# Retention attention and a Mish MLP on one core: q and k of the first two tiles by batch, a quarter of w_in on another queue, G2 of tile 0 moved up

## The chip, the core and the metric

The kernel runs on one core of a Trainium2 chip. The core has five engines, each with its own instruction queue that runs in order: TensorE (PE, matrix products; its weight loads are PEld), VectorE (DVE), ScalarE (ACT), GpSimd (POOL) and SyncE (SP, which only issues transfers here). Transfers between the chip's memory and the core's on-chip memory (DMAs) are issued by SP, POOL or ACT and are carried out by 16 DMA engines. Matrix results go to PSUM, eight banks of 128 partitions x 2 KB.

The metric is the device time of one execution in microseconds (us). Before the change it is 351.88 us, the median of 3 runs (351.87 to 352.25).

## The reference

Eight batches, eight heads, 576 positions, head size 64. Attention with a decay, no softmax; then an MLP over all 4608 tokens.

```python
scores = scale * np.matmul(q, k.transpose(0, 1, 3, 2))
Dmat = np.where(rel >= 0, gamma[:, None, None] ** rel[None, :, :], 0.0)
attn = np.matmul(scores * Dmat, v)                   # 8, 8, 576, 64
x = attn.transpose(0, 2, 1, 3).reshape(4608, 512)
h = x @ w_in                                         # 512 x 2048
out = (h * np.tanh(softplus(h))) @ w_out             # Mish, 2048 x 512
```

## The kernel before

Tokens are cut into 36 chunks of 128, and four chunks make a tile: nine tiles, t = 0 to 8. Tiles 0 and 1 hold chunk 0 of each of the eight batches, which needs no earlier state and has a path of its own. Chunk n >= 8 (N0 = 8) is a later chunk of a batch and takes its past from a running state.

For a tile, G1 (`g1`, 16 calls of 4 products of 128x128 by 128x512) computes h from w_in, and ACT applies Mish into `gT`. G2 (`g2`, 16 calls of 4 products) multiplies `gT` by w_out: four groups s of 128 tokens, each in four parts of w_out. The result is copied to `res` and stored (`store`). I call a call of `g1` or `g2`, four products, a unit.

The program orders every instruction by hand (`manual_schedule`): each engine's queue is the order in which Python emits it. What counts around the change:

- **First tiles.** `load_first(t)` fetches q and k of four batches into `stage` (name gT) by 16 DMAs of 128 KB, one per head and tensor, over all 128 partitions, then four v DMAs of 256 KB; all on SP. `f_cast` makes bf16 of a pair of heads (8 per tile), `f_transpose` turns it on PE through PSUM, `f_scores` multiplies and DVE applies the decay, `f_v` casts v, `f_out` multiplies by v into `xT`, `f_state` scales v for the state (POOL) and `f_k` reorders k inside on-chip memory by four DMAs per batch on SP. For tile 0 `keep_warm` puts products of zeros between them.
- **Weights.** `load_w_in(i)` and `load_w_out(i)` load a quarter each (1 MB read, 512 KB written as bf16) on POOL's queue. The second `load_first` waits for a write into `stage` behind tile 0's output (L433).
- **Order of the tiles.** G1 of tile 0 (L355) has the transposes and scores of tile 1 between its units from f = 6 on; then `f_out` of tile 1; then five chunk loads; G1 of tile 1; G2 of tile 0 with the attention of chunks 8 to 11 (tile 2); and from there a loop over t = 2 to 8 in which unit i of G1 of tile t and unit i of G2 of tile t - 1 take turns, with the attention of the next tile between them.
- **Chunks.** `load(n)` issues k on POOL (cast to bf16 on its way) and q, v on SP. The steps: P scales q (DVE), V scales v (POOL, L264), T transposes q and k, S computes the scores (L286) and masks them on DVE, `state` updates the running state, O adds the state's part and the chunk's own (L336, L341). T runs on PE with a copy by ACT for n < NPE = 12, and as a DMA transpose issued by SP (L276) from n = 12 on.
- **Buffers.** `io` has five (PF) of qraw and of vraw; `hp` two banks, `sc` two of two banks, `st` and `ops` one each; `res` three.

Of the kernel before, what the change touches and what calls it, by code (L numbers as in the profile page):

```python
# [17 lines left out]
def kernel(  # L18
# [25 lines left out]
    nF = d_ff // P  # L44
    KC = d_model // P
    NCH = 4
    NPE = 12
    PF = 5


# [44 lines left out]
    v0 = {}  # L95

    def load_first(t):
        for p in range(NP):
            for dst, src in ((qf, q), (kf, k)):
                for h in (2 * p, 2 * p + 1):  # L100
                    nc.sync.dma_start(  # L101
                        out=dst[:, h, :],
                        in_=src[ds(4 * t, 4), h, 0:P, :].rearrange("b (g r) d -> g b (r d)", r=4))
        for b in range(4 * t, 4 * t + 4):
            v0[b] = io.tile([P, H, D], F32, name="vraw")
            nc.sync.dma_start(out=v0[b], in_=v[b, :, 0:P, :].rearrange("h p d -> p h d"))

    load_first(0)

    zeros = consts.tile([P, 512], BF16)  # L110
    nc.vector.memset(zeros, 0.0)  # L111
# [64 lines left out]
    def f_transpose(t, p, copies):  # L176
        if t == 0:
            tps = [ps_h.tile([P, 4, P], BF16, name="hp") for _ in range(2)]
        else:
            both = ps_sc.tile([P, 2, 8, P], BF16, name="sc")  # L180
            tps = [both[:, i, 0:4] for i in range(2)]
        for i, name in enumerate(("qb", "kb")):
            out_t = first.tile([P, 4, P], BF16, name=name + "T", bufs=2)
            for r in range(4):
                nc.tensor.transpose(tps[i][:, r, :],
                                    fst[t][name][:, r, ds(2 * p, 2), :].rearrange("p h d -> p (h d)"), ident)
            copies[i](out_t.rearrange("p b (g r) -> p b g r", r=4),
                      tps[i].rearrange("p r (g b) -> p b g r", b=4))
            fst[t][name, p] = out_t

    def f_scores(t, p):
# [16 lines left out]
    def f_out(t, b, copy):  # L208
        if b == 0:
            xts[t] = xp.tile([P, KC, NCH * P], BF16, name="xT")  # L210
        vb = fst[t]["vb"][b]
        pool, name = ((ps_st, "st"), (ps_o, "ops"))[b % 2]
        ot = pool.tile([P, NP, P], F32, name=name)
        for p in range(NP):
            for e in range(2):
                nc.tensor.matmul(ot[ds(64 * e, 64), p, :], lhsT=vb[:, 2 * p + e, :],
                                 rhs=fst[t]["sm", p][:, e, b, :],
                                 start=(p == 0), stop=True, skip_group_check=True)
        copy(xts[t][:, :, ts(b, P)], ot)
# [7 lines left out]
    def f_k(t, b):  # L227
        n = 4 * t + b
        k0[n] = first.tile([P, H, D], BF16, name="k0", bufs=B)
        for r in range(4):  # L230
            nc.sync.dma_start(out=k0[n][ds(r, 32, step=4)].rearrange("p h d -> p (h d)"),  # L231
                              in_=fst[t]["kb"][ds(b, 32, step=4), r].rearrange("p h d -> p (h d)"))

    def load(n):
        if n >= n_chunks:
            return
        b, c = chunks[n]
        qr = io.tile([P, H, D], F32, name="qraw")  # L240
        vr = io.tile([P, H, D], F32, name="vraw")
        qks = io.tile([P, 2, H, D], BF16, name="qks", bufs=9)
        live[n] = {"q": qr, "v": vr, "qks": qks}
        if n == N0:
            nc.vector.memset(qr[0:1, 0, 0:1], 0.0)
        for t, src, queue in ((qks[:, 1], k, nc.gpsimd), (qr, q, nc.sync), (vr, v, nc.sync)):
            if c < 4:
                queue.dma_start(  # L248
                    out=t, in_=src[b, :, ds(P * c, P), :].rearrange("h p d -> p h d"))
            else:  # L250
                for e in range(2):
                    queue.dma_start(
                        out=t[ds(64 * e, 64)],
                        in_=src[b + e, :, ds(512, 64), :].rearrange("h p d -> p h d"))

# [103 lines left out]
    def g2(t, i):  # L359
        s, part = divmod(i, 4)  # L360
        if t == nT - 1:
            s = (s + 3) % 4
        if part == 0:
            if (t == nT - 1 or t == 0) and s % 2:
                outs[t] = ps_h.tile([P, d_model], F32, name="hp")
            else:
                outs[t] = ps_o.tile([P, d_model], F32, name="ops")
        ops = outs[t]
        for f in range(4 * part, 4 * part + 4):
            nc.tensor.matmul(ops, lhsT=gts[t][:, f, ts(s, P)], rhs=w_out_t[:, f, :],  # L370
                             start=(f == 0), stop=(f == nF - 1))
        if part == 3:
            store(t, s, ops, nc.scalar.copy if t == 0 else nc.vector.tensor_copy)

    def g2_last(t, s):
        b, c = chunks[NCH * t + s]
# [26 lines left out]
    dve, act, pool = nc.vector.tensor_copy, nc.scalar.copy, nc.gpsimd.tensor_copy  # L403


    f_cast(0, 0, 0, dve)
    f_cast(0, 0, 1, pool)
    for p in range(1, NP):
        f_cast(0, p, 0, pool)
        f_cast(0, p, 1, pool)  # L410
        if p == 2:
            make_masks()
    load_w_in(0)
    keep_warm(8)
    for p in range(NP + 1):
        if p < NP:
            f_transpose(0, p, (act, act))
            keep_warm(3)
        if p > 0:
            f_scores(0, p - 1)  # L420
            keep_warm(2)
    f_v(0, 0, pool)
    f_v(0, 1, act)
    load_w_in(1)
    f_v(0, 2, pool)
    f_v(0, 3, dve)
    for b in range(4):
        f_out(0, b, (dve, act)[b % 2])
        if b < 3:
            keep_warm_b = 0  # L430
    load_w_in(2)
    load_w_in(3)
    nc.vector.memset(stage[0:1, 0, 0, 0:1], 0.0)  # L433
    load_first(1)
    for b in range(4):
        f_state(0, b)
        f_k(0, b)
    for i in range(4):
        load_w_out(i)


    for p in range(NP):
        f_cast(1, p, 0, pool)
        f_cast(1, p, 1, pool)
    for b in range(4):
        f_v(1, b, pool)
    for b in range(4):
        f_state(1, b)
        f_k(1, b)
    for f in range(nF):  # L450
        if f in (6, 8, 10, 12):
            f_transpose(1, (f - 6) // 2, (dve, dve))
        if f in (8, 10, 12, 14):
            f_scores(1, (f - 8) // 2)
        g1(0, f)
    for b in range(4):
        f_out(1, b, dve)


    for n in range(N0, N0 + PF):  # L460
        load(n)
    for f in range(nF):
        g1(1, f)
        if f == 8:
            state(N0)
    att(N0, "PV")
    for i in range(nF):
        n, w = N0 + i // 4, i % 4
        if w == 0:
            att(n, "T")  # L470
        elif w == 1:
            if i > 4:
                att(n - 1, "O")
        elif w == 2:
            att(n, "S")
            state(n + 1)
        else:
            att(n + 1, "PV")
            load(n + PF)
            state(n + 1)  # L480
        g2(0, i)
    att(3 * NCH - 1, "O")
    queued = [3 * NCH + PF - 1]

    def more_loads(upto):
        for _ in range(2):
# [4 lines left out]
    for t in range(2, nT + 1):  # L491
        for i in range(nF):
            n, w = NCH * (t + 1) + i // 8 * 2, i % 8
            if t == nT:
                pass
            elif n == 3 * NCH:
                steps = {0: ((n, "T"), (n + 1, "PV")), 1: ((n + 1, "T"), (n, "K")),
                         3: ((n, "S"), (n + 1, "S"), (n + 1, "K")), 2: ((n + 2, "PV"),), 4: ((n + 3, "PV"),),
                         6: ((n + 1, "K"), (n, "O"), (n + 1, "O"), (n + 3, "K"), (n + 2, "T")),
                         7: ((n + 3, "T"),)}  # L500
                for m, step in steps.get(w, ()):
                    if step == "K":
                        state(m)
                        continue
                    att(m, step)
                    if step == "PV":
                        more_loads(m + PF)
            else:
                if w == 0:
                    att(n, "S")  # L510
                    att(n + 1, "S")
                    state(n + 1)
                if w in (0, 2):
                    att(n + 2 + w // 2, "PV")
                    more_loads(n + 2 + w // 2 + PF)
                elif w in (1, 3):
                    att(n + 2 + w // 2, "T")
                elif w == 4:
                    state(n + 3)
                    att(n, "O")  # L520
                    att(n + 1, "O")
                    state(n + 3)
                elif w == 6:
                    state(n + 3)
            if t < nT:
                g1(t, i)
            if t < nT or i < 12:
                g2(t - 1, i)
    g2_last(nT - 1, 2)

# [29 lines left out]
```

## Time and profile before

One execution was profiled. Its instructions span 352.2 us, and it took 353.91 us with what lies around them; the runs without a profile have the median 351.88.

| | busy us | share of the span |
|---|---|---|
| PE | 311.0 | 88% |
| ACT | 130.5 | 37% |
| DVE | 110.0 | 31% |
| POOL | 86.7 | 25% |

| group | count | mean |
|---|---|---|
| G1 products, L355 | 546 | 390 ns |
| G2 products, L370 | 492 + 61 | 381, 379 ns |
| Mish, L357 | 144 | 597 ns |
| score mask, L290 | 28 | 1216 ns |
| chunk T copied by ACT, L274 | 4 | 1015 ns |

Of the 41 us in which PE has nothing to do, most lie ahead of 150 us. A product's 390 ns is not its cost: products are pipelined, and a unit of four follows the last by 0.86 us. "DMA" in the slices of the page is the mean busy share of the 16 DMA engines, and a name such as `DMA qkT<-qks` is a transfer by its target and source.

### The profile page before, as it was taken

The numbers are of one execution on the slowest core, as the hardware profiler recorded it, in microseconds if no ns is written. First come the engines' busy times: TensorE is split into PE (matmuls) and PEld (weight loads), VectorE is DVE, ScalarE is ACT, GpSimd is POOL, SyncE is SP. The second block draws the span as 40 slices with busy tenths as digits, with TensorE's granted clock in tenths as the row PEclk, the third lists the DMA queues.
The fourth block names the chain that finished last, engine by engine and source line by source line (L and its number), as shares of the span: only waits on it lengthen the run. The fifth ranks groups of instructions, "written<-read, shape, count | busy, mean of one in ns | idle before, by whom it ended". The sixth has DMA issues, their size and how long they took to land.

```text
span 352.2 us, 5825 instructions
## 1 busy us (share of the span) xinstructions
PE 311.0 (88%) x2342; PEld 152.0 (43%) x2380; DVE 110.0 (31%) x156; ACT 130.5 (37%) x241; POOL 86.7 (25%) x112
## 2 busy tenths in 40 slices
PE   5927678979970999999999999999999999999995
PEld 2413333435430445444544445454545454444444
DVE  2330364014521352424252525244242423200021
ACT  7414132745420244353434344343435243333300
POOL 4682249017451144040404031320201000000000
PEclk9987898999996799999999999999999999999999
DMA  4999974989999999995979788991723220020022
GB/s 148 212 202 216 257 171 67 111 162 203 214 223 203 188 134 181 123 191 92 180 126 147 164 117 170 130 173 68 152 44 78 67 54 30 32 58 33 30 61 89
DMA packets 140123, 46.65 MB, mean 132 GB/s; under 512 B 126144, under 2 KB 135616, under 8 KB 140096
## 3 DMA queue, kind: packets, MB, share of 16 engines
q1 hardware_dynamic: 105504, 38.16, 51.0%
q0 software_dynamic: 34448, 8.00, 26.5%
q8 instruction: 18, 0.29, 0.4%
q10 hardware_dynamic: 144, 0.13, 0.1%
q14 instruction: 9, 0.07, 0.1%
HBM read 37.49 MB, written 9.44 MB: 133 GB/s over the span
## 4 chain that ended last, share of the span: by engine, by line
PE 66%; DMA 17%; SPq 11%; issue 2%; ACT 2%; DVE 1%; POOL 0%; ACTq 0%; DVEq 0%; POOLq 0%
PE ops L370 28%; PE hp L355 25%; DMA qkT<-qks 8%; SPq L231 6%; DMA gT<-in_q_dram 5%; PE hp L370 4%; SPq L101 4%; DMA vraw<-in_v_dram 3%; PE sc L286 2%; PE st L318 2%; ACT ssb L322 1%; PE sc L336 1%; DMA qraw<-in_q_dram 1%; PE sc L341 1%; PE hp L381 1%
## 5 line engine op out<-in xcount | busy, mean ns | idle before, releaser
L355 PE MATMUL hp<-xT,w_in_t 128*128 128x512 bf16 x546 | 145.8, 390 | 5.3 <-issue 2.2
L357 ACT ACTIVATE gT<-hp 128x512 bf16<-128x512 f32 x144 | 86.0, 597 | 149.2 <-PE hp L355 143.6
L370 PE MATMUL ops<-w_out_t,gT 128*128 128x512 bf16 x492 | 126.8, 381 | 0.4 <-PE st L318 0.2
L355 PEld LDWEIGHTS <-w_in_t 128*128 128x128 bf16 x576 | 55.1, 100 | 68.7 <-issue 9.3
L370 PEld LDWEIGHTS <-gT 128*128 128x128 bf16 x560 | 54.1, 98 | 64.7 <-issue 1.9
L389 DVE COPY res<-ops 128x512 f32<-128x512 f32 x29 | 20.1, 692 | 147.0 <-PE ops L370 140.4
L264 POOL TENSOR_TENSOR vs<-vraw,gv 128x512 bf16<-128x512 f32 x28 | 29.3, 1048 | 148.0 <-issue 89.7
L322 ACT ACTIVATE ssb<-st,diag 128x256 bf16<-128x256 f32 x64 | 26.8, 470 | 34.2 <-PE st L318 34.2
L290 DVE TENSOR_TENSOR sm<-sc,mask 128x1024 bf16<-128x1024 f32 x28 | 33.1, 1216 | 18.7 <-PE sc L286 18.7
L258 DVE TENSOR_TENSOR qks<-qraw,gq 128x512 bf16<-128x512 f32 x28 | 18.2, 682 | 18.0 <-DMA qraw<-in_q_dram 18.0
L248 POOL DMA_DIRECT2D qks<-in_k_dram x25 | 23.1, 931 | 2.2 <-PE st L318 2.2
L345 DVE CAST xT<-sc 128x512 bf16<-128x512 f32 x28 | 18.2, 686 | 10.7 <-PE sc L341 10.6
L286 PE MATMUL sc<-qkT 64*128 64x128 bf16 x224 | 10.0, 224 | 10.6 <-DMA qkT<-qks 10.6
L370 PE MATMUL hp<-w_out_t,gT 128*128 128x512 bf16 x61 | 14.7, 379 | 0.4 <-issue 0.3
L286 PEld LDWEIGHTS <-qkT 64*128 64x128 bf16 x224 | 6.5, 96 | 18.1 <-DMA qkT<-qks 11.7
L160 PE MATMUL ops<-zeros 128*128 128x512 bf16 x27 | 11.0, 529 | 1.3 <-DVE zeros L111 1.3
L199 DVE TENSOR_TENSOR sm<-sc,dmask 128x1024 bf16<-128x1024 f32 x8 | 9.7, 1218 | 7.7 <-PE sc L197 7.7
L336 PE MATMUL sc<-qkT,ssb 128*64 128x128 bf16 (+1 forms) x256 | 11.2, 215 | 0.0
L341 PE MATMUL sc<-sm,vs 128*64 128x128 bf16 x224 | 10.9, 219 | 0.0
L336 PEld LDWEIGHTS <-ssb 128*64 128x64 bf16 x256 | 7.8, 111 | 2.5 <-issue 2.5
L225 POOL TENSOR_TENSOR v0s<-vraw,gv 128x512 bf16<-128x512 f32 x8 | 8.4, 1072 | 1.5 <-DMA vraw<-in_v_dram 1.5
L318 PE MATMUL st<-vs,qks 128*64 128x64 bf16 x192 | 7.7, 202 | 1.0 <-ACT ssb L322 0.5
(71 smaller groups left out, 116.5 us busy)
## 6 DMA issues: line engine op xcount, KB each, us to landing
vraw<-in_v_dram SPq DMA_DIRECT2D x33, 256.0 KB, 4.5
out_dram<-res SPq DMA_DIRECT2D x31, 256.0 KB, 2.1
qraw<-in_q_dram SPq DMA_DIRECT2D x25, 256.0 KB, 3.7
qks<-in_k_dram POOLq DMA_DIRECT2D x25, 128.0 KB, 5.7
gT<-in_q_dram SPq DMA_DIRECT2D x16, 128.0 KB, 5.0
gT<-in_k_dram SPq DMA_DIRECT2D x16, 128.0 KB, 4.3
w_in_t<-in_moe_w_in_dram POOLq DMA_DIRECT2D x4, 512.0 KB, 9.6
w_out_t<-in_moe_w_out_dram POOLq DMA_DIRECT2D x4, 512.0 KB, 13.8
```

What stands on the lines that cost most here:

```text
L231: nc.sync.dma_start(out=k0[n][ds(r, 32, step=4)].rearrange("p h d -> p (h d)"), in_=fst[t]["kb"][ds(b, 32, step=4), r].rearrange("p h d -> ...
L248: queue.dma_start(out=t, in_=src[b, :, ds(P * c, P), :].rearrange("h p d -> p h d"))
L258: nc.vector.tensor_tensor(live[n]["qks"][:, 0], live[n]["q"], gq[:, c, :].unsqueeze(2).to_broadcast([P, H, D]), op=OP.mult)
L264: nc.gpsimd.tensor_tensor(vs, live[n]["v"], gv[:, c, :].unsqueeze(2).to_broadcast([P, H, D]), op=OP.mult)
L286: nc.tensor.matmul(sc[:, e, p, :], lhsT=qk[r, 1, p, :], rhs=qk[r, 0, p, :], start=True, stop=True)
L290: nc.vector.tensor_tensor(sm.rearrange("p e n i -> p (e n) i"), sc.rearrange("p e n i -> p (e n) i"), m.unsqueeze(1).to_broadcast([P, 2 * ...
L322: nc.scalar.activation(ssb[:, :, e, :], st, AX.Copy, scale=diag[:, e:e + 1])
L336: nc.tensor.matmul(ot[ds(64 * e, 64), p, ds(i0, iw)], lhsT=st_sb[bb, cc][:, p, e, :], rhs=qk[:, 0, p, ds(i0, iw)], start=(i0 == 0 and p == ...
L355: nc.tensor.matmul(hp, lhsT=w_in_t[:, c, ts(f, P)], rhs=xts[t][:, c, :], start=(c == 0), stop=(c == KC - 1))
L357: nc.scalar.activation(gts[t][:, f, :], hp, AX.Mish)
L370: nc.tensor.matmul(ops, lhsT=gts[t][:, f, ts(s, P)], rhs=w_out_t[:, f, :], start=(f == 0), stop=(f == nF - 1))
L389: copy(ot, ops)
```

## The change

- Of tiles 0 and 1, q and k are fetched by half of the heads, by tensor and by batch: 16 DMAs of 128 KB, each into 32 partitions. The rows of a tile are then ordered by batch, so the transposes' copies read `(b g)` instead of `(g b)`, and `f_k` is one DMA per batch instead of four.
- The first quarter of w_in comes in f32 by four DMAs on SP after v of tile 0, into free qraw buffers, and DVE casts it. The other three stay on POOL.
- q, k of tile 1 are issued on SP behind that, with no write that holds them back. v of tile 1 is issued on POOL.
- Tile 0's q casts go to DVE for even pairs; tile 1's eight casts go to DVE. Fewer `keep_warm`.
- G1 of tile 0 runs without anything in it. G2 of tile 0 follows at once (`g2_first`): by part of w_out first, then by group s, with four open results in `hp`, `hp`, `ops`, `st`; tile 1's transposes and scores lie between its units. Then `f_v` and `f_out` of tile 1.
- G1 of tile 1 and the first half of G2 of tile 1 (24 units) then have the attention of chunks 8 to 11 between them. The loop at t = 2 has 16 units of G1 and the 8 that remain of G2 of tile 1.
- NPE is 16: chunks 12 to 15 are transposed on PE too.
- All chunk loads (q, k, v) are issued on POOL.

```diff
-    NPE = 12
+    NPE = 16
     def load_first(t):
-        for p in range(NP):
+        for half in range(2):
+            hs = ds(4 * half, 4)
             for dst, src in ((qf, q), (kf, k)):
-                for h in (2 * p, 2 * p + 1):
+                for b in range(4):
                     nc.sync.dma_start(
-                        out=dst[:, h, :],
-                        in_=src[ds(4 * t, 4), h, 0:P, :].rearrange("b (g r) d -> g b (r d)", r=4))
+                        out=dst[ds(32 * b, 32), hs, :],
+                        in_=src[4 * t + b, hs, 0:P, :].rearrange("h (g r) d -> g h (r d)", r=4))
...
+            (nc.gpsimd if t else nc.sync).dma_start(out=v0[b], in_=v[b, :, 0:P, :].rearrange("h p d -> p h d"))
     load_first(0)
+    load_first_v(0)
+    w0 = []
+    for c in range(KC):
+        w0.append(io.tile([P, 512], F32, name="qraw"))
+        nc.sync.dma_start(out=w0[c], in_=w_in_r[:, c, 0:512])
...
-        for r in range(4):
-            nc.sync.dma_start(out=k0[n][ds(r, 32, step=4)].rearrange("p h d -> p (h d)"),
-                              in_=fst[t]["kb"][ds(b, 32, step=4), r].rearrange("p h d -> p (h d)"))
+        nc.sync.dma_start(out=k0[n].rearrange("p h d -> p (h d)"),
+                          in_=fst[t]["kb"][ds(32 * b, 32)].rearrange("p r h d -> p r (h d)"))
...
-        for t, src, queue in ((qks[:, 1], k, nc.gpsimd), (qr, q, nc.sync), (vr, v, nc.sync)):
+        for t, src in ((qr, q), (qks[:, 1], k), (vr, v)):
             if c < 4:
-                queue.dma_start(
+                nc.gpsimd.dma_start(
...
+    def g2_first(part, s):
+        if part == 0:
+            pool, name = ((ps_h, "hp"), (ps_h, "hp"), (ps_o, "ops"), (ps_st, "st"))[s]
+            outs[0, s] = pool.tile([P, d_model], F32, name=name)
+        for f in range(4 * part, 4 * part + 4):
+            nc.tensor.matmul(outs[0, s], lhsT=gts[0][:, f, ts(s, P)], rhs=w_out_t[:, f, :],
+                             start=(f == 0), stop=(f == nF - 1))
+        if part == 3:
+            store(0, s, outs[0, s], nc.scalar.copy if s % 2 else nc.vector.tensor_copy)
...
+    load_first(1)
     keep_warm(8)
...
+    for i in range(1, 4):
+        load_w_in(i)
     for b in range(4):
         f_out(0, b, (dve, act)[b % 2])
+        dve(w_in_t[:, b, 0:512], w0[b])
...
     for p in range(NP):
-        f_cast(1, p, 0, pool)
-        f_cast(1, p, 1, pool)
+        f_cast(1, p, 0, dve)
+        f_cast(1, p, 1, dve)
+    for f in range(nF):
+        g1(0, f)
     for b in range(4):
+        f_k(1, b)
+    load(N0)
+    first_steps = {0: (f_transpose, 0), 1: (f_transpose, 1), 3: (f_scores, 0), 4: (f_scores, 1),
+                   6: (f_transpose, 2), 7: (f_transpose, 3), 9: (f_scores, 2), 11: (f_scores, 3)}
+    for i in range(nF):
...
+        g2_first(i // 4, i % 4)
+    for b in range(4):
+        f_v(1, b, act if b % 2 else pool)
+    for b in range(4):
+        f_out(1, b, (dve, act)[b % 2])
+    for b in range(4):
+        f_state(1, b)
+        load(N0 + 1 + b)
+    att(N0, "PV")
+    for u in range(24):
+        j, w = divmod(u, 4)
...
+        elif w == 3 and j < 4:
+            att(N0 + j, "T")
...
+        if u < nF:
+            g1(1, u)
+        else:
+            g2(1, u - nF)
...
+            if t == 2:
+                if i % 2:
+                    g2(1, 8 + i // 2)
```

More of the change, by code (lines that the diff above doesn't have):

```diff
@@ L97, in load_first, with load_first_v @@
     def load_first(t):
-        for p in range(NP):
+        for half in range(2):
+            hs = ds(4 * half, 4)
             for dst, src in ((qf, q), (kf, k)):
-                for h in (2 * p, 2 * p + 1):
+                for b in range(4):
                     nc.sync.dma_start(
-                        out=dst[:, h, :],
-                        in_=src[ds(4 * t, 4), h, 0:P, :].rearrange("b (g r) d -> g b (r d)", r=4))
+                        out=dst[ds(32 * b, 32), hs, :],
+                        in_=src[4 * t + b, hs, 0:P, :].rearrange("h (g r) d -> g h (r d)", r=4))
+    def load_first_v(t):
         for b in range(4 * t, 4 * t + 4):
             v0[b] = io.tile([P, H, D], F32, name="vraw")
-            nc.sync.dma_start(out=v0[b], in_=v[b, :, 0:P, :].rearrange("h p d -> p h d"))
+            (nc.gpsimd if t else nc.sync).dma_start(out=v0[b], in_=v[b, :, 0:P, :].rearrange("h p d -> p h d"))
     load_first(0)
+    load_first_v(0)
[3 more added lines that the diff above has]
+        nc.sync.dma_start(out=w0[c], in_=w_in_r[:, c, 0:512])
     zeros = consts.tile([P, 512], BF16)
@@ L187, in f_transpose @@
             copies[i](out_t.rearrange("p b (g r) -> p b g r", r=4),
-                      tps[i].rearrange("p r (g b) -> p b g r", b=4))
+                      tps[i].rearrange("p r (b g) -> p b g r", b=4))
             fst[t][name, p] = out_t
@@ L211, in f_out @@
         vb = fst[t]["vb"][b]
-        pool, name = ((ps_st, "st"), (ps_o, "ops"))[b % 2]
-        ot = pool.tile([P, NP, P], F32, name=name)
+        if t == 0:
+            pool, name = ((ps_st, "st"), (ps_o, "ops"))[b % 2]
+            ot = pool.tile([P, NP, P], F32, name=name)
+        else:
+            if b % 2 == 0:
+                fst[t]["ot"] = ps_sc.tile([P, 2, NP, P], F32, name="sc")
+            ot = fst[t]["ot"][:, b % 2]
         for p in range(NP):
@@ L243, in load @@
         live[n] = {"q": qr, "v": vr, "qks": qks}
-        if n == N0:
-            nc.vector.memset(qr[0:1, 0, 0:1], 0.0)
-        for t, src, queue in ((qks[:, 1], k, nc.gpsimd), (qr, q, nc.sync), (vr, v, nc.sync)):
+        for t, src in ((qr, q), (qks[:, 1], k), (vr, v)):
             if c < 4:
-                queue.dma_start(
+                nc.gpsimd.dma_start(
                     out=t, in_=src[b, :, ds(P * c, P), :].rearrange("h p d -> p h d"))
@@ L251, in load @@
                 for e in range(2):
-                    queue.dma_start(
+                    nc.gpsimd.dma_start(
                         out=t[ds(64 * e, 64)],
@@ L363, in g2 @@
         if part == 0:
-            if (t == nT - 1 or t == 0) and s % 2:
+            if t == nT - 1 and s % 2:
                 outs[t] = ps_h.tile([P, d_model], F32, name="hp")
@@ L372, in g2 @@
         if part == 3:
-            store(t, s, ops, nc.scalar.copy if t == 0 else nc.vector.tensor_copy)
+            store(t, s, ops, nc.vector.tensor_copy)
+    def g2_first(part, s):
[7 more added lines that the diff above has]
+            store(0, s, outs[0, s], nc.scalar.copy if s % 2 else nc.vector.tensor_copy)
     def g2_last(t, s):
@@ L403 @@
     dve, act, pool = nc.vector.tensor_copy, nc.scalar.copy, nc.gpsimd.tensor_copy
[L406 to L409, printed above, removed]
+    for p in range(NP):
+        f_cast(0, p, 0, pool if p % 2 else dve)
         f_cast(0, p, 1, pool)
-        if p == 2:
-            make_masks()
-    load_w_in(0)
+    load_first(1)
     keep_warm(8)
@@ L417 @@
             f_transpose(0, p, (act, act))
-            keep_warm(3)
+            keep_warm(2)
         if p > 0:
             f_scores(0, p - 1)
-            keep_warm(2)
     f_v(0, 0, pool)
     f_v(0, 1, act)
-    load_w_in(1)
     f_v(0, 2, pool)
-    f_v(0, 3, dve)
+    f_v(0, 3, act)
+    for i in range(1, 4):
+        load_w_in(i)
     for b in range(4):
         f_out(0, b, (dve, act)[b % 2])
[L429 to L434, printed above, removed]
+        dve(w_in_t[:, b, 0:512], w0[b])
     for b in range(4):
@@ L439 @@
         load_w_out(i)
+    load_first_v(1)
+    make_masks()
     for p in range(NP):
-        f_cast(1, p, 0, pool)
-        f_cast(1, p, 1, pool)
+        f_cast(1, p, 0, dve)
+        f_cast(1, p, 1, dve)
+    for f in range(nF):
+        g1(0, f)
     for b in range(4):
-        f_v(1, b, pool)
+        f_k(1, b)
+    load(N0)
+    first_steps = {0: (f_transpose, 0), 1: (f_transpose, 1), 3: (f_scores, 0), 4: (f_scores, 1),
+                   6: (f_transpose, 2), 7: (f_transpose, 3), 9: (f_scores, 2), 11: (f_scores, 3)}
@@ L447 @@
+    for i in range(nF):
+        if i in first_steps:
+            step, p = first_steps[i]
+            if step is f_transpose:
+                step(1, p, (dve, act))
+            else:
+                step(1, p)
+        g2_first(i // 4, i % 4)
[3 more added lines that the diff above has]
+        f_out(1, b, (dve, act)[b % 2])
     for b in range(4):
         f_state(1, b)
[L449 to L465, printed above, removed]
+        load(N0 + 1 + b)
     att(N0, "PV")
-    for i in range(nF):
-        n, w = N0 + i // 4, i % 4
+    for u in range(24):
+        j, w = divmod(u, 4)
         if w == 0:
[L470 to L476, printed above, removed]
-        else:
[L478 to L481, printed above, removed]
@@ L482 @@
-    att(3 * NCH - 1, "O")
-    queued = [3 * NCH + PF - 1]
+            if 0 < j:
+                att(N0 + j, "PV") if j < 5 else None
+                load(N0 + j + PF - 1) if j < 5 else None
+            if 2 <= j < 6:
+                att(N0 + j - 2, "O")
+        elif w == 3 and j < 4:
+            att(N0 + j, "T")
+        elif w == 1 and 1 <= j < 5:
+            att(N0 + j - 1, "S")
+            state(N0 + j - 1)
+        elif w == 2 and j < 5:
+            state(N0 + max(j - 1, 0))
+        if u < nF:
+            g1(1, u)
+        else:
+            g2(1, u - nF)
@@ L485, in more_loads @@
+    queued = [3 * NCH + PF]
     def more_loads(upto):
@@ L526 @@
                 g1(t, i)
-            if t < nT or i < 12:
+            if t == 2:
+                if i % 2:
+                    g2(1, 8 + i // 2)
+            elif t < nT or i < 12:
                 g2(t - 1, i)
```

## The prediction

> **What bounds the kernel now.** First the slices of the page, to see where PE, the busiest engine, is not full: up to the 17th of 40 slices, some 150 us; behind them it is at 9 throughout.
>
> ```profile
> PE   5927678979970999999999999999999999999995
> PEclk9987898999996799999999999999999999999999
> ```
>
> Then the stages, PE's busy time in three windows. The loop over t = 2 runs from 98.55 to 143.58; the next two lines are whole tiles (32 units each).
>
> ```profile
> 98.55:143.58 45.03, 34.52 (x268) 16.57 (x271) 12.28 (x16) 13.74 (x26) 13.20 (x15) 0.89 1.30 185
> 143.58:176.97 33.39, 32.18 (x262) 15.83 (x266) 12.27 (x16) 13.74 (x26) 8.25 (x9) 1.00 0.93 143
> 160.74:193.13 32.39, 31.68 (x261) 15.69 (x265) 12.26 (x16) 12.91 (x24) 8.19 (x9) 1.00 1.02 140
> ```
>
> A tile costs 32.4 us and is PE all through. In the chain of waits a unit takes 0.86 us, so 32 units are 27.6 and a tile's attention 4.8. At t = 2 the same work takes 45.0: 12.6 are lost. Third, PE's timeline, for what it waited for ("[idle before <-who ended it]"):
>
> ```profile
> 25.01 0.64 PE L216 MATMUL st<-sm,vb 128*64 128x128 bf16 x8 [5.32 <-DVE xT L219]
> ...
> 27.55 6.29 PE L355 MATMUL hp<-xT,w_in_t 128*128 128x512 bf16 x22 [0.22 <-issue]
> 35.56 0.40 PE L185 MATMUL sc<-ident,qb 128*128 128x128 bf16 x4 [1.72 <-POOL qb L173]
> ...
> 76.19 0.62 PE L273 MATMUL sc<-ident,qks 128*128 128x128 bf16 x8 [2.64 <-DVE qks L258]
> ...
> 109.01 0.61 PE L286 MATMUL sc<-qkT 64*128 64x128 bf16 x8 [5.12 <-DMA qkT<-qks]
> 114.36 0.61 PE L286 MATMUL sc<-qkT 64*128 64x128 bf16 x8 [4.74 <-DMA qkT<-qks]
> ```
>
> The 12.6 are two DMA transposes, with the half clock that follows (0.55 from 110 to 120). The front is another matter: from 26.75 to 57.5 PE does one G1 (13.8 us of units) and tile 1's first attention, and waits for tile 1's q and k. Last, SP's and POOL's queues, for why data come late:
>
> ```profile
> 47.95 22.96 SPq L231 DMA_DIRECT2D k<-kb  x32
> 71.01 1.57 SPq L248 DMA_DIRECT2D qraw<-in_q_dram  x1
> ```
>
> 32 small DMAs hold SP for 23 us, and the first chunk's q is issued only at 71.
>
> **The change, part by part.** All times are on the profiled execution.
>
> *Tile 0's loads.* Still 16 q, k DMAs of 128 KB, one per 0.64 us, 2.6 to 2.9 us from issue to landing: the first half of k lands at 8.1, the last k at 13.2. What 32 partitions cost in place of 128 the trace does not show. From below, nothing: the issue is the limit. From above, twice the 0.64: 10.3 us. The nearest row, 128 KB into 64 partitions (L252, 3.4 us to landing, against 3.7 for 256 KB into 128), shows a small load as no slower, so I take 0 and leave the 10.3 to a rival.
>
> [...]
>
> POOL's last cast moves from 13.95 to 15.1 (kb, then qb, kb at 0.61 after 13.2), a loss of 1.1 that lies beside v.
>
> *v and w_in.* v lands at 14.9, 16.2, 17.3 and only 23.9 for the fourth, because w_in's DMAs issued from 13.90 on take the engines. Now w_in waits on POOL for the third v's cast (17.9), so the fourth v lands one step later, 18.5. The first w_in quarter follows on SP: a quarter alone takes 2.55 (landings 25.0 to 30.1, two steps), shared at most twice that: 21.0 to 23.6, I take 22.5. DVE's casts are four at 0.43 (row L173), the last behind the landing. G1 of tile 0 starts at 23, not 26.75.
>
> *Weights and tile 1's q, k share the engines from 22.5 on.* In the trace, sharing, a quarter took 4.1 (w_out, 33.9 to 46.3) and a q or k DMA 0.92 (33.4 to 47.2, 15 steps), 1.1 in its middle. So w_in's last three land at 25, 29 and 33, the last k between 37 and 40, w_out at 37, 40, 42.5 and 45, v of tile 1 at 1.2 each by 50. G1 of tile 0 ends 3.45 (four units) after 33, at 37 with a little for the clock, which was at 0.68 from 20 to 30.
>
> *G2 of tile 0.* 16 units 13.8, four transposes at 0.45, four scores at 0.33: 16.9. DVE's queue has all eight casts of tile 1 ahead of the first qbT copy, so the first scores wait for the last k, three casts (1.3) and 0.69: 39 to 42, where PE would come at 40.5. I take 1. End: 55. Before, this was not done at 57.5.
>
> *To G1 of tile 1.* The fourth result's copy by ACT needs a third `res` back, whose store left some 2 us earlier (landings 2.1 in the median): a wait of 0 to 1.6. Behind it on ACT lie two vb casts (0.63) and two xT copies (0.59), and G1 waits for the last: 0.6 + 1.3 + 1.2 + 1.6 = 4.7. Start 60, where before it was 57.5. So 16 units, 13.8, are won here and 2.5 given back. At this place the clock fell for some 3.4 us before (0.88 in 50 to 60); I keep that, 1.7.
>
> *24 units with attention.* 20.7 + 4.8 + four transposes 1.8 = 27.3. ACT has in four units four Mish (0.597), a copy of 1.015 and a state (0.84): 4.2 of PE's 5.1; it fits, but bunched, with two `hp` banks. Cost 0 to 4 (one copy per chunk); I take 1.5. The 2.64 at 76 has gone, for q no longer stands behind `f_k`. End: 60 + 1.7 + 27.3 + 1.5 = 90.5.
>
> *Loads on POOL.* Three issues per chunk:
>
> ```profile
> L248 POOL DMA_DIRECT2D qks<-in_k_dram x25 | 23.1, 931 | 2.2 <-PE st L318 2.2
> L264 POOL TENSOR_TENSOR vs<-vraw,gv 128x512 bf16<-128x512 f32 x28 | 29.3, 1048 | 148.0 <-issue 89.7
> ```
>
> 2.8 + 1.05 is 3.85 of the 8.1 us that a chunk takes PE. At the start it is tight: from 49 POOL has four v0s and four loads, one of which waits for ACT's vb (58), then vs of chunks 8 and 9, at 67 and 68. PE needs the first in O of chunk 8, eight units and some attention after 61.7: 70. Cover 3; without it every us counts.
>
> *t = 2.* 16 + 8 units 20.7, attention 4.8, four PE transposes 1.8 for the 12.6 lost: 27.3 and 0.5 for small gaps. End 118.3, where before it was 143.58: 25.3 less. Behind it the order is the old one and already full; SP carries less there. I take 0; from below -1 (the gaps from 143.58 to 176.97 against the tile after), from above +3 (a transposed chunk late, as the 0.50 at 144.48, at each tile).
>
> **Sum.** 352.2 - 25.3 = 326.9. The median of the runs is 0.3 below the profiled span, so 327 (the profiled execution itself, 353.91, would be near 329). With no cold clock, no bunching and no wait for `res` or k it is 6 less: 320.5; with k and w_out 3 late and 4 for ACT, 334.
>
> **Rivals.**
>
> *The front is late.* Each us that tile 1's last k or w_out comes after 41 delays G2 of tile 0. For: queues there were full before (mean share above 1). Against: the bytes up to 50 are the same, and v no longer stands in w_in's way. With half the rate into 32 partitions tile 0 is 10.3 later, 337, and part of tile 1's 16 times 0.92 more comes on top: 334 to 346, at 340.
>
> *Only the transposes' stall goes.* If PE with G1 and attention waits as long as G2's early units gained, 12.6 less 1.8 remain: 341.4. For: two banks, a fuller ACT. Against: 4.2 of 5.1.
>
> *POOL becomes the bound, and it is slower than before.* All loads stand in order behind V's waits. From 50 on POOL has 28 chunks, and 60 us follow the last scores (291.6 of 352.2). It passes 352 once a chunk takes (352 - 110)/28 = 8.65, an issue 2.5 us. At 3 us an issue: 50 + 28 x 10.05 + 60 = 391. Against: 0.93 in 25 rows, and 4.46 for five in a row.
>
> **How the numbers follow.** Forecast 0.66 (own range 320 to 334), late front 0.20, transposes only 0.06, POOL 0.07, no change 0.01. The range 320 to 341 holds the forecast, two thirds of the late front and little of the rest: near 0.8. Within 0.2% is what a measurement of this kernel can't tell from no change. Faster: 0.66 + 0.20 + 0.06 = 0.92; same 0.01; slower 0.07.
>
> **What would show it.** G1 of tile 0 starts near 23 and ends near 37; G2 of tile 0 ends near 55; G1 of tile 1 starts near 60; no PE wait for qkT of 4 to 5 us remains; the t = 2 loop takes some 28; PE's busy time stays near 311 and its idle falls from 41 to some 16. Wrong, if POOL's issues take over 1.5 us, if q or k of tile 1 lands after 45, or if whole tiles behind 120 take more than 33.

## The result, and the profile after

The changed kernel takes 334.53 us, the median of 4 runs (333.42 to 335.18), beside 352.06 us (351.87 to 352.66) of the kernel before on the same chip. The ratio is 0.950, with the interval 0.947 to 0.953. The profiled execution took 335.18 us and its instructions span 333.5. PE's busy time hardly moved (311.0 to 309.7); its idle time fell from 41 to 24 us, not to 16.

The slices of the page:

```profile
PE   5839788699999999999999999999999999999996
PEclk9969999879999999999999999999999999999999
```

A slice is 8.3 us here. PE is full from the ninth slice on, some 67 us, where before it was from the fourteenth, some 115 (its row reads 7 and 0 in the 12th and 13th slice and 9 from there; the prediction's 17th and 150 are misread). The long dip of the old loop over t = 2 has gone. What is left lies in the first eight slices.

The stages, in three windows of busy time (start and end, length; then PE, PEld, DVE, ACT and POOL, each with its count, PE's granted clock, the DMA share and GB/s). The first holds the 24 units with the attention of chunks 8 to 11, the second the loop over t = 2, the third a whole tile:

```profile
67.28:97.78 30.50, 30.22 (x264) 14.69 (x264) 12.31 (x14) 16.80 (x30) 26.93 (x31) 0.94 0.95 165
97.78:126.12 28.34, 27.82 (x281) 14.67 (x280) 11.57 (x15) 18.01 (x32) 20.15 (x23) 1.00 0.83 133
126.12:158.83 32.71, 32.42 (x266) 15.82 (x266) 12.26 (x16) 13.74 (x26) 14.90 (x16) 1.00 1.10 164
```

The loop over t = 2 took 45.03 before and takes 28.34 now: 8 of its units moved ahead (6.9 us) and 9.8 us more are gone, the waits less the four added PE transposes. In all three stages PE is busy all but half a microsecond. So most of the time by which the kernel misses the forecast lies ahead of 67. PE's timeline there:

```profile
23.33 12.15 PE L365 MATMUL hp<-xT,w_in_t 128*128 128x512 bf16 x48 [3.23 <-DVE xT L232]
...
41.49 0.38 PE L193 MATMUL sc<-ident,kb 128*128 128x128 bf16 x4 [1.75 <-DVE qbT L195]
...
43.81 0.38 PE L193 MATMUL sc<-ident,kb 128*128 128x128 bf16 x4 [0.85 <-DVE qbT L195]
...
50.39 0.38 PE L193 MATMUL sc<-ident,kb 128*128 128x128 bf16 x4 [0.78 <-DVE qbT L195]
...
52.65 0.38 PE L193 MATMUL sc<-ident,kb 128*128 128x128 bf16 x4 [0.78 <-DVE qbT L195]
...
64.14 1.05 PE L229 MATMUL sc<-sm,vb 128*64 128x128 bf16 x16 [2.12 <-ACT vb L213]
...
67.28 3.57 PE L365 MATMUL hp<-xT,w_in_t 128*128 128x512 bf16 x8 [0.67 <-ACT xT L232]
```

Four times in G2 of tile 0 PE comes to k's transposes and waits for DVE to have copied q's out of the same `sc` tile. These four are 4.2 us, the largest group of waits in the profile. The first is longer than the others because DVE's queue has three of tile 1's casts, behind the last k's landing at 39.6, ahead of that copy:

```profile
39.74 0.43 DVE L181 CAST kb<-gT 128x512 bf16<-128x512 f32 x1 [4.03 <-DMA gT<-in_k_dram]
...
40.76 0.68 DVE L195 COPY qbT<-sc 128x512 bf16<-128x512 bf16 x1
```

Then PE waits 2.1 us for v's cast by ACT. The last row of PE's timeline is a half clock (0.50 granted from 64.2 to 71.0): eight products took 3.57 us, where they take 1.89 at full clock.

SP's and POOL's queues, at the places that were shown of before:

```profile
31.87 11.49 SPq L243 DMA_DIRECT2D k<-kb  x8
```

```profile
L258 POOL DMA_DIRECT2D qks<-in_k_dram x24 | 21.6, 899 | 3.0 <-DMA w_out_t<-in_moe_w_out_dram 3.0
```

The reordering of k holds SP for 11.5 us instead of 23, and POOL's issues cost 0.90 to 0.93 us, as before.

### The profile page after: what moved, and what is told of

Read it like the earlier page. It is cut to its first block, busy times and chain, and to the rows that moved or that the text cites. A ratio compares the mean times of both kernels' runs of the same rounds, so it can differ in the third digit from the quotient of the medians.

```text
span 333.5 us, 5849 instructions
## 1 busy us (share of the span) xinstructions
PE 309.7 (93%) x2400; PEld 151.5 (45%) x2400; DVE 117.2 (35%) x162; ACT 137.6 (41%) x252; POOL 136.0 (41%) x167
## 4 chain that ended last, share of the span: by engine, by line
PE 81%; DMA 9%; SPq 3%; DVE 2%; ACT 2%; issue 1%; DVEq 0%; ACTq 0%
PE hp L365 34%; PE ops L380 30%; DMA gT<-in_k_dram 6%; PE st L328 3%; PE sc L296 2%; PE hp L380 2%; PE hp L391 2%; DMA qraw<-in_moe_w_in_dram 2%; ACT ssb L332 2%; SPq L102 1%; DMA gT<-in_q_dram 1%; PE sc L346 1%; SPq L109 1%; PE hp L402 1%; PE sc L283 1%
## 5 line engine op out<-in xcount | busy, mean ns | idle before, releaser
L365 PE MATMUL hp<-xT,w_in_t 128*128 128x512 bf16 x576 | 147.6, 386 | 4.3 <-DVE xT L232 3.2
L367 ACT ACTIVATE gT<-hp 128x512 bf16<-128x512 f32 x144 | 86.1, 598 | 126.1 <-PE hp L365 124.6
L380 PE MATMUL ops<-w_out_t,gT 128*128 128x512 bf16 x464 | 117.9, 379 | 0.3 <-DVE res L410 0.3
L365 PEld LDWEIGHTS <-w_in_t 128*128 128x128 bf16 x576 | 53.8, 99 | 67.5 <-issue 4.0
L380 PEld LDWEIGHTS <-gT 128*128 128x128 bf16 x496 | 48.3, 98 | 58.4 <-issue 1.0
L258 POOL DMA_DIRECT2D qraw<-in_q_dram x24 | 22.4, 933 | 54.0 <-DVE qks L268 52.2
L274 POOL TENSOR_TENSOR vs<-vraw,gv 128x512 bf16<-128x512 f32 x28 | 29.7, 1074 | 12.6 <-PE sc L351 12.4
L332 ACT ACTIVATE ssb<-st,diag 128x256 bf16<-128x256 f32 x64 | 26.8, 470 | 16.9 <-PE st L328 16.9
L258 POOL DMA_DIRECT2D vraw<-in_v_dram x24 | 21.8, 908 | 6.0 <-issue 3.3
L258 POOL DMA_DIRECT2D qks<-in_k_dram x24 | 21.6, 899 | 3.0 <-DMA w_out_t<-in_moe_w_out_dram 3.0
L268 DVE TENSOR_TENSOR qks<-qraw,gq 128x512 bf16<-128x512 f32 x28 | 20.5, 767 | 0.0
L262 POOL DMA_DIRECT2D qraw<-in_q_dram x8 | 5.6, 703 | 14.9 <-DVE qks L268 14.9
L284 ACT COPY qkT<-sc 128x1024 bf16<-128x1024 bf16 x8 | 8.1, 1011 | 6.0 <-PE sc L283 5.9
L296 PE MATMUL sc<-qkT 64*128 64x128 bf16 x224 | 9.0, 217 | 0.0
```

What stands on the lines that cost most here:

```text
L258: nc.gpsimd.dma_start(out=t, in_=src[b, :, ds(P * c, P), :].rearrange("h p d -> p h d"))
L268: nc.vector.tensor_tensor(live[n]["qks"][:, 0], live[n]["q"], gq[:, c, :].unsqueeze(2).to_broadcast([P, H, D]), op=OP.mult)
L274: nc.gpsimd.tensor_tensor(vs, live[n]["v"], gv[:, c, :].unsqueeze(2).to_broadcast([P, H, D]), op=OP.mult)
L296: nc.tensor.matmul(sc[:, e, p, :], lhsT=qk[r, 1, p, :], rhs=qk[r, 0, p, :], start=True, stop=True)
L332: nc.scalar.activation(ssb[:, :, e, :], st, AX.Copy, scale=diag[:, e:e + 1])
L365: nc.tensor.matmul(hp, lhsT=w_in_t[:, c, ts(f, P)], rhs=xts[t][:, c, :], start=(c == 0), stop=(c == KC - 1))
```

## The experiments

Twelve kernels ran, in three groups; each group has its own runs of the kernel before, and the changed kernel ran again in the third. Its ratio was 0.950 at first and 0.957 (0.954 to 0.959) in the third group, so between groups only differences of some 1% are read. Smaller ones are read within a group, or from a stage in the traces. Edits are to the changed kernel unless said otherwise.

### 1. q's copy behind k's transposes

```diff
             for r in range(4):
                 nc.tensor.transpose(tps[i][:, r, :], ...
-            copies[i](out_t.rearrange(...), tps[i].rearrange(...))
             fst[t][name, p] = out_t
+        for i, name in enumerate(("qb", "kb")):
+            copies[i](fst[t][name, p].rearrange(...), tps[i].rearrange(...))
```

> Changed kernel, but in f_transpose all eight transposes of a pair come ahead of the two copies, in both first tiles; nothing else. My theory: of the 7 us that G2 of tile 0 ends later than I predicted, 4.2 are PE waiting, four times, for DVE's copy of qbT before it writes k's transposes into the other half of the same tile; so the four waits go and the kernel takes 334.5 - 4 = 330.5 us (329.5 to 331.5). Rival: the q, k and w_out landings are the limit there (last k 39.6, w_out 39.9 to 51.0), so the waits move to the first scores or to the parts of G2 and the time stays within 1 us of 334.5.

Measured: 329.91 us against 351.18, ratio 0.939 (0.935 to 0.943), span 329.5. All four waits are gone, as in the first two transposes of PE's timeline:

```profile
39.77 0.39 PE L193 MATMUL sc<-ident,qb 128*128 128x128 bf16 x4
40.00 0.39 PE L193 MATMUL sc<-ident,kb 128*128 128x128 bf16 x4
```

G2 of tile 0 with its transposes and scores runs from 39.8 to 57.3, 17.5 us instead of 22.25, and G1 of tile 1 starts at 62.6 instead of 67.3. The theory holds: transposes of k write the other half of the tile that DVE reads, and with the copy emitted ahead of them they wait for it. Emitted behind both, nothing waits. PE's timeline then shows what is next:

```profile
60.11 0.64 PE L230 MATMUL sc<-sm,vb 128*64 128x128 bf16 x16 [2.44 <-ACT vb L214]
```

### 2. v's casts ahead of the last results of G2

```diff
+        if i == 12:
+            for b in range(4):
+                f_v(1, b, act if b % 2 else pool)
         g2_first(i // 4, i % 4)
-    for b in range(4):
-        f_v(1, b, act if b % 2 else pool)
```

> Changed kernel, but tile 1's four v casts are emitted before the last four units of G2 of tile 0 instead of behind them. Theory: ACT's two casts then no longer stand behind the copy of the fourth result, which waits for a store to land; G1 of tile 1 starts some 2.5 us earlier (64.8 in place of 67.3), and with a shorter gap PE may keep its clock, worth up to 1.8 more: 330 to 332. Rival: the xT copies of ACT still stand behind that copy, and POOL's chunk loads set the pace of what follows: within 1 us of 334.5.

Measured: 332.16 us, ratio 0.946 (0.943 to 0.950), span 330.7. ACT casts at 52.9 and 54.6. Its copy into `res` still waits 2.1 us for a store, but nothing of PE stands behind it any more:

```profile
62.06 0.64 PE L229 MATMUL sc<-sm,vb 128*64 128x128 bf16 x16 [0.79 <-DVE xT L232]
...
64.57 1.89 PE L365 MATMUL hp<-xT,w_in_t 128*128 128x512 bf16 x7 [0.67 <-ACT xT L232]
```

From v's first products to G1 it is 3.7 us instead of 5.7, and G1 starts at full clock. So the wait for a `res` buffer was real and reached PE through the two casts queued behind it on ACT, as the prediction had it in "To G1 of tile 1".

### 3. The DMA transposes back for chunks 12 to 15

```diff
-    NPE = 16
+    NPE = 12
```

> Changed kernel with NPE back at 12: chunks 12 to 15 are transposed by DMAs on SP. Theory of the prediction: the 12.6 us lost in the loop at t = 2 belonged to the DMA transposes, and the PE transposes are worth that less 1.8, so the time goes back by 8 to 11: 343 to 345. Rival: it was SP's queue, full of loads and stores, that held the transposes, and it is empty now, so the time goes back by at most 3: 333 to 337.

Measured: 339.92 us, ratio 0.968 (0.964 to 0.972), span 338.3: 4 to 6 us back. PE's timeline:

```profile
104.67 0.61 PE L296 MATMUL sc<-qkT 64*128 64x128 bf16 x8 [3.56 <-DMA qkT<-qks]
106.68 0.61 PE L296 MATMUL sc<-qkT 64*128 64x128 bf16 x8 [1.40 <-DMA qkT<-qks]
```

with a half clock from 103.9 to 110.7. Neither expectation fits: the stall came back smaller than it was (5.0 of waits instead of 9.9). SP issued these transposes at 98.5 and 100.1 with nothing ahead of them, and they landed 6.1 and 6.6 us later, while POOL's chunk loads of the same time took 5.6 to 8.8. So what is left of the delay is the time from issue to landing, not SP's queue.

### 4. q and v of the chunks back on SP

```diff
-        for t, src in ((qr, q), (qks[:, 1], k), (vr, v)):
+        for t, src, queue in ((qr, q, nc.sync), (qks[:, 1], k, nc.gpsimd), (vr, v, nc.sync)):
...
-                nc.gpsimd.dma_start(
+                queue.dma_start(
```

> Changed kernel with q and v of the chunks back on SP, k on POOL. Theory: the loads' move to POOL is worth little by itself now that f_k has 8 DMAs and not 32; POOL has a slack of some 3 us at chunk 8, SP gives it more: 333 to 336. Rival: on SP the loads stand behind stores and wait for G2 again, and chunks come late: 338 or more.

Measured: 338.29 us (334.94 to 338.75), ratio 0.962 (0.956 to 0.968), span 337.0. Up to the first scores of t = 3 it is 0.85 us ahead of the changed kernel. Then the loop over t = 3 begins. In the changed kernel SP issues its two first transposes at 116.9 and 118.4; here loads stand ahead of each, and the second goes at 121.8, to land at 128.2 instead of 125.9. SP's queue in the changed kernel, then SP's and PE's in this one:

```profile
116.91 2.80 SPq L286 DMA_TRANSPOSE qkT<-qks  x2
```

```profile
118.76 1.34 SPq L286 DMA_TRANSPOSE qkT<-qks  x1
120.20 0.53 SPq L258 DMA_DIRECT2D qraw<-in_q_dram  x1
120.84 0.82 SPq L258 DMA_DIRECT2D vraw<-in_v_dram  x1
121.83 3.46 SPq L286 DMA_TRANSPOSE qkT<-qks  x1
```

```profile
128.28 0.40 PE L296 MATMUL sc<-qkT 64*128 64x128 bf16 x8 [2.61 <-DMA qkT<-qks]
```

The wait of 2.6 and the half clock behind it (128.9 to 132.4, 1.7 us) are 4.3, less 0.85: the 3.5 by which the span is longer. By the ratios the move of the loads to POOL would be worth 2 to 4 us, where the prediction had nothing ("SP carries less there"). That price is not shown: the interval overlaps that of the changed kernel in the third group, and one of the four runs, 334.94, was as fast as the changed kernel. The changed kernel's profile in the third group (span 337.7) has a wait of 1.8 us for a transposed chunk too, at 144.0, with the loads on POOL. What the traces do show is the place in SP's queue and the 3.5 us in the profiled execution.

### 5. NPE = 16 alone, in the kernel before

> Kernel before with NPE at 16 alone: chunks 12 to 15 are transposed on PE. Theory: the 12.6 us lost in its loop at t = 2 are the two DMA transposes and the half clock behind them, and four PE transposes cost 1.8: 10.8 less, 0.969 of before (0.965 to 0.974). Rival: the loads of these chunks stand in SP's queue and are as late as the transposes, so the wait moves to PE's transposes: 0.98 to 1.0 of before.

Measured: 343.43 us against 350.30, ratio 0.981 (0.978 to 0.985), span 342.4. A window over its loop, and its timeline ahead of the loop:

```profile
100.59:134.86 34.27, 33.52 (x292) 17.18 (x297) 13.30 (x16) 17.30 (x30) 11.62 (x13) 1.00 1.27 186
```

```profile
75.19 1.04 PE L273 MATMUL sc<-ident,qks 128*128 128x128 bf16 x8 [5.03 <-DVE qks L258]
```

The loop fell from 45.03 to 34.27, by 10.8: the stall less the PE transposes, of which three lie in this window and the fourth just ahead of it. But the loop began 2 us later: G1 of tile 1 started 1.7 earlier, and PE then waited 5.0 us, not 2.6, for the first chunk's q. This q stands behind the 32 reordering DMAs on SP, and a half clock from 72.6 to 79.4 sets in during the wait. Behind the loop 1.1 were won, so the profiled span is 9.8 less (10.76 - 2.04 + 1.08). By the medians it is 6.9, for the profiled execution of the kernel before, 353.91, was 3.6 above the median of this group, and that of the edited kernel 0.7 above its own. The size was right where it was computed, and part of it was given back at another place.

### 6. The order of the batches, and the old layout

Alone, the order 0, 2, 1, 3 of the batches' DMAs:

```diff
-                for b in range(4):
+                for b in (0, 2, 1, 3):
```

> Changed kernel, but the four q or k DMAs of a half are issued for batches 0, 2, 1, 3 in place of 0, 1, 2, 3, so that neighbours in the queue write to different halves of the partitions. If 16 DMAs into 32 partitions each are held by the part of on-chip memory that they write (in the changed kernel they are issued each 0.475 us but land each 0.655), tile 0's last k lands earlier than 12.6, at 11 or so. If not, at 12.6 as before. The time is the same in both (within 1.5 us), for w_in and tile 1's k end this stage.

And, in another kernel, q and k by head as before, with `f_k` in four DMAs per batch; the rest as changed:

```diff
-        for half in range(2):
+        for p in range(NP):
...
-                        out=dst[ds(32 * b, 32), hs, :],
+                        out=dst[:, h, :],
```

> Changed kernel with the by-batch layout alone undone: q, k of tiles 0 and 1 by head into 128 partitions, f_k by 32 DMAs of 32 KB. Theory: the layout is worth little by itself: tile 0's last k lands at 13.2 in place of 12.6, f_k's 23 us on SP hold up only stores now, and tile 1's pairs arrive one by one, which DVE's casts like: 333 to 336. Rival: f_k's small DMAs hold up the stores of tile 0's results and by them G1 of tile 1: 338 or more.

Measured: 334.68 us, ratio 0.956 (0.952 to 0.960), with the last k of tile 0 landed at 11.85 instead of 12.61; and 335.49 us, ratio 0.958 (0.955 to 0.962), with the last k at 13.31. Neither differs from the changed kernel (0.950 and 0.957) by more than the groups do. So the layout by itself costs little, as the prediction took it, but not for its reason; see the last section.

### 7. The casts of w_in's first quarter on ACT

```diff
-        dve(w_in_t[:, b, 0:512], w0[b])
+        act(w_in_t[:, b, 0:512], w0[b])
```

> Changed kernel with the four casts of the first w_in quarter on ACT. In the changed kernel two of DVE's casts take 3.4 us together, where one is 0.43, while POOL runs its four v0s. Theory: DVE and POOL keep each other waiting there; on ACT a cast takes 0.63 or less than 1, G1 of tile 0 starts 1 to 2 us earlier (21.5 to 22.5), and the time stays within 1 us of the changed kernel's, since w_in's last quarter (35.8) ends the stage. Rival: w_in's DMAs on POOL start late because of it (first packet 4.0 us after the issue, 2.8 before), then w_in's last lands at 34.5 or earlier and a us is won.

Measured: 335.62 us, ratio 0.960 (0.955 to 0.965), span 332.3. G1 of tile 0 starts at 21.2 instead of 23.3, but then waits for w_in:

```profile
21.17 3.61 PE L365 MATMUL hp<-xT,w_in_t 128*128 128x512 bf16 x15 [1.00 <-ACT xT L232]
26.75 3.63 PE L365 MATMUL hp<-xT,w_in_t 128*128 128x512 bf16 x16 [1.97 <-DMA w_in_t<-in_moe_w_in_dram]
```

The start is 2.2 earlier and G1 ends at 38.46, only 0.9 earlier: here each quarter of w_in that comes from POOL makes PE wait (2.0, 0.55 and 0.44 us), and the last of them, landed at 35.0, sets the end.

### 8. Combinations, beside the changed kernel

The changed kernel as it is:

> The changed kernel once more, unchanged, beside the next three on the same chip, for the kernel before differs by some us from chip to chip (348.8 to 353.3 so far): 333 to 336, 0.947 to 0.956 of before.

Edits 1 and 2 together:

> Changed kernel with the transposes ahead of the copies and with the v casts early (the two edits tried alone). Theory: the two waits stand one behind the other on PE's path, so their gains add: 3.7 + 2.5 less than the changed kernel, 327 to 330. Rival: with G2 of tile 0 4 us earlier, v of tile 1 (landing 52 to 56) and POOL's chunk loads behind it come last, and the second gain is lost: 330 or more.

The batches' order and the casts on ACT together:

> Changed kernel with batches in the order 0, 2, 1, 3 and the w_in casts on ACT, nothing else. Theory: G1 of tile 0 ends 1 to 2 us earlier, as w_in's last quarter lands at 34 or so, but the waits in G2 of tile 0 stay, and tile 1's last k (38 to 39) and DVE's casts hold the first of them: 0 to 1.5 less than the changed kernel.

Edits 1 and 2, both of these, a fourth `res` buffer, and tile 1's products by v ahead of their copies:

```diff
-        copy(xts[t][:, :, ts(b, P)], ot)
+        if t == 0:
+            copy(xts[t][:, :, ts(b, P)], ot)
+        elif b == 3:
+            for bb, (o, cp) in enumerate(fst[t]["late"] + [(ot, copy)]):
+                cp(xts[t][:, :, ts(bb, P)], o)
+        else:
+            fst[t].setdefault("late", []).append((ot, copy))
...
-        ot = op.tile([P, d_model], F32, name="res")
+        ot = op.tile([P, d_model], F32, name="res", bufs=4)
```

> All that helped or seemed to, on the changed kernel: transposes ahead of copies, v casts early, four res buffers, the products of f_out of tile 1 ahead of its copies (PE waits twice 0.8 for the copy of the other half of the same tile), batches in the order 0, 2, 1, 3, the w_in casts on ACT. Theory: G1 of tile 1 starts at 58 to 60 in place of 67.3 and everything behind follows until POOL's loads are late: 325 to 328. Rival: POOL, which ends its first vs at 74 in the changed kernel, sets the time of the first O step, and no more than e8 is reached: 328 to 330.

Measured, against 351.18 of the kernel before:

| kernel | us | ratio | interval |
|---|---|---|---|
| as changed | 336.47 | 0.957 | 0.954 to 0.959 |
| edits 1 and 2 | 328.59 | 0.936 | 0.934 to 0.938 |
| order, casts on ACT | 334.59 | 0.952 | 0.950 to 0.955 |
| all of them | 329.40 | 0.938 | 0.935 to 0.942 |

Edits 1 and 2 add up: 7.9 us off the changed kernel, and the lowest median of all. The two edits at the front bring 1.9: G1 of tile 0 starts at 20.3, w_in's last quarter lands at 33.7, and G1 ends at 37.25 instead of the 40.0 of this group's changed kernel. On top of edits 1 and 2 nothing is left of that. G1 of tile 1 does start at 58.6, 1.5 ahead of the kernel with edits 1 and 2 alone, but POOL is not ready for it. POOL's and PE's timelines of the kernel with all edits:

```profile
68.67 2.06 POOL L281 TENSOR_TENSOR vs<-vraw,gv 128x512 bf16<-128x512 f32 x2
```

```profile
69.79 0.41 PE L358 MATMUL sc<-sm,vs 128*64 128x128 bf16 x8 [2.11 <-POOL vs L281]
```

and a half clock from 71.0 to 74.4 follows. In the kernel with edits 1 and 2 the same multiply is done at about the same time, and PE waits 0.4 for it; in the changed kernel it had 3 us to spare.

## Why the prediction was right, and where its terms were off

The side was right and 334.5 lies in the stated range, but 0.5 above the forecast's own upper end of 334, in the part that was held open for a late front. The gain is 17.5 us where 25 were forecast. Every step of the forecast has its time in the trace; the last column is what the step itself added:

| step | forecast | measured | more |
|---|---|---|---|
| G1 of tile 0 starts | 23 | 23.3 | 0.3 |
| w_in's last quarter lands | 33 | 35.8 | |
| G1 of tile 0 ends | 37 | 39.35 | 2.0 |
| G2 of tile 0, length | 18 | 22.25 | 4.25 |
| from it to G1 of tile 1 | 5 | 5.7 | 0.7 |
| 24 units with attention | 30.5 | 30.5 | 0 |
| loop over t = 2 | 27.8 | 28.3 | 0.5 |
| first scores of t = 3 | 118.3 | 126.1 | 7.8 |
| from there to the end | 208.6 | 207.4 | -1.2 |

The sum closes: 326.9 + 7.8 - 1.2 = 333.5, the span.

**The step that failed is "I take 1" in "G2 of tile 0".** It asked when the last k arrives and put a wait of some 1 us at the first scores. The last k did land at 39.6, within the 37 to 40 given, but the first scores waited for nothing of it, for three units lie ahead of them. The wait was ahead of that: k's transposes waited for q's copy, four times, 4.2 us. Some 0.9 of it, in the first of the four, belongs to the last k and its casts, which the 1 was for (in the changed kernel's profile of the third group, where that k landed 1.2 ahead of the end of G1, the first wait is 0.85 too). The other 3.3 had no term in the sum. The trace of before held their price, in two rows of PE's timeline that the working passed over:

```profile
42.31 0.38 PE L185 MATMUL sc<-ident,kb 128*128 128x128 bf16 x4 [0.85 <-DVE qbT L187]
...
49.89 0.38 PE L185 MATMUL sc<-ident,kb 128*128 128x128 bf16 x4 [0.78 <-DVE qbT L187]
```

Four times 0.8 would have been 3.2. Experiment 1 took the four away and the stage fell from 22.25 to 17.5, by 4.8, where the four waits themselves were 4.2. Of the 0.6 that remain against the 16.9 of the sum, 0.4 are four units that stand ahead of scores and take 0.96 instead of 0.86.

**The second is the end of G1 of tile 0.** The forecast set it by w_in's last quarter, with "a little for the clock". The three quarters were put at 25, 29 and 33 and landed at 27.7, 31.7 and 35.8; the pitch of 4 was right, the first landing 2.7 late. But PE waited only 0.4 us for the last of them. More came from the clock: it was at 0.50 from 19.8 to 26.6, so the first 3.3 us of G1 lost 1.65. So even with w_in at 33, G1 would have ended at an estimated 38.8 (23.3 + 13.8 of units + 1.65), and only some 0.5 of the 2.0 is w_in's.

Why w_in was late is not settled. Its first bytes moved 4.0 us after POOL's issue, where before it was 2.8; with the casts on ACT it was still 3.8, so DVE's casts are not the main reason. In the seven profiles with the front as changed the last quarter landed between 34.5 and 36.5. With the casts on ACT it was 35.0, within that. With the order 0, 2, 1, 3 it was 33.5 and 33.7, and 34.7 in the kernel with all edits, so the order may bring a us.

**What held.** The stall of the transposes: 12.6 less 1.8 was computed, and experiment 5 shows 10.8 in the loop. The 24 units: 30.5, with the 1.7 for the clock (3.57 less 1.89). The wait for `res` and the two casts behind it: 5.7 for the 4.7, and experiment 2 shows the mechanism. POOL: 0.90 to 0.93 us an issue, and vs of chunk 8 done at 74.4, O of chunk 8 on PE at 77.7, so a cover of 3.3, where 3 was given, though both came 6 to 8 us later than forecast; whole tiles behind 120 take 32.4 to 32.7.

**What was luck.** That 334.5 lies in the range at all: the part of it above 334 was there for a late front, and what filled it was mostly another wait. The 1.5 for ACT in the 24 units is right only as a number. PE is idle for 0.28 us of that stage. In the kernel with edits 1 and 2, where the stage runs at full clock, it takes 29.4 us with PE busy for 28.7, against the 27.3 of units, attention and transposes. So the 1.5 is PE's own work, in part units ahead of scores or O that take 0.95 to 0.97 instead of 0.86, and no bunching on ACT. The 1.2 won behind the loop had been put at 0. And two bounds do not follow from the terms: 326.9 less 1.7, 1.5, 1.6 and 1 is 321.1, not 320.5, and 3 for k and 2.5 more for ACT give 332.4, not 334.

**The rivals.** "The front is late" did not come about as it was meant. The last k of tile 1 came at 39.6, and though w_out landed at 39.9 to 51.0 and v of tile 1 at 52.1 to 55.7, later than forecast, PE waited for neither. 32 partitions did not halve the rate: tile 0's q and k landed every 0.61 us, where before it was 0.65, and the last k at 12.6, where the forecast had 13.2. Late was w_in, by 2.8. "Only the transposes' stall goes" fell: from the changed kernel NPE = 12 takes back 4 to 6 us of 17.5. "POOL becomes the bound" fell for this kernel, but its place was right: it is what ends the gain of the fastest front in experiment 8. No run takes back the early G2 of tile 0 alone, nor the quarter of w_in on SP alone; their share of the 17.5 is read from the steps of the trace.

**An edit that was costed at nothing.** The loads' move from SP to POOL gains nothing up to t = 2, but without it a DMA transpose at t = 3 stands behind loads on SP, and the profiled execution lost 3.5 us there (experiment 4). The forecast took those stages as full already. Whether the move is what keeps them so in most executions is not shown.

## What to carry to other kernels

Where two halves of one buffer are filled and emptied in turns, look at where the copy of the first half is emitted: between the two fills it stalled the producer here (four waits, 4.2 us), behind both it did not (experiment 1), and a row with such a wait in the old profile prices it. Look also at what an in-order engine has queued behind a copy that needs a buffer back from a store: two casts behind such a copy cost PE 2 us here, and moving them up was free. And when the front of a kernel gets faster, look up the engine whose queue starts at a fixed landing: POOL's cover here was 3 us, and the gain ended there.

## What the runs showed of the chip

- **Small DMAs into 32 partitions.** They are issued faster than those into 128 (0.43 us against 0.60, every 0.47 against 0.65), but landed every 0.61, and issue to landing grew from 2.57 to 4.70 over 16 of them; before it was 2.5 to 3.0 throughout. (The 0.655 of experiment 6's expectation is too high; eight profiles with this order give 0.61 to 0.64.) So the transfer was the limit, not the issue as the prediction had it. With the batches in the order 0, 2, 1, 3 the pitch of landings was 0.58 in all three profiles. Why the order counts is not shown.
- **Casts on DVE beside multiplies on POOL.** In the changed kernel's timeline two of w_in's casts took 3.43 us, while POOL multiplied; tile 1's casts of this size take 0.42 to 0.43 on DVE in the same trace:

```profile
19.24 3.43 DVE L446 CAST w_in_t<-qraw 128x512 bf16<-128x512 f32 x2
```

```profile
19.11 4.45 POOL L238 TENSOR_TENSOR v0s<-vraw,gv 128x512 bf16<-128x512 f32 x4
```

  With the casts on ACT (experiment 7) each took 0.62 us, and POOL's four multiplies 4.07 instead of 4.45. So beside each other both took longer; what holds them back is not shown.
- **POOL's issues behind POOL's older DMAs.** Six issues on POOL began 0.3 to 0.6 us after the landing of an older DMA with which they share no data (one of the six rows names ACT as what ended the wait), as this row of the changed kernel's timeline:

```profile
44.37 0.88 POOL L258 DMA_DIRECT2D qks<-in_k_dram  x1 [3.05 <-DMA w_out_t<-in_moe_w_out_dram]
```

  At each of the six, seven DMAs of POOL's were under way, with the new one eight, and in the whole trace never more. That it is a limit of the queue is argued from this; no run varied it.
- **The half clock moves.** During a wait of PE or soon after one its granted clock fell to 0.50, for 3.4 or 6.8 us (in the kernel before from 57.6 to 61.0 and from 23.5 to 30.3), and in the kernel before once for 10.2 (from 108.8 to 119.1). Where it fell differed between executions of one kernel: from 64.2 to 71.0 in the first profile of the changed kernel, from 66.1 to 69.5 in the other. The other also has a wait of 1.8 us for a transposed chunk at 144.0 that the first lacks. So a single profile is good to some 2 us at such a place.
